# Idle products: their operand zeroed ahead of the masks, more of them at the begin, and a new order table

## The chip, the core and the metric

The kernel runs on one core of a Trainium2 chip. The engines are named PE (TensorE, matmul), DVE (VectorE), ACT (ScalarE), POOL (GpSimd) and SP (SyncE, which here only issues DMAs). The metric is device time in microseconds, the median of several runs.

## What is computed

Three layers follow each other: windowed attention, a gated two-layer product with a shift by one position, and a convolution gate with two products. Batch 4, 8 heads, 576 positions, head size 64; all in float32 (the arrays of q, k, v), weights given as float64 words that the kernel turns into float32 itself.

```python
# attention, window 64
scores = q @ k.transpose(0, 1, 3, 2) / 8
rel = pos[:, None] - pos[None, :]
scores = where((rel >= 0) & (rel < 64), scores, -1e9)
attn = exp(scores - max(scores)); attn = attn / (sum(attn) + 1e-9)
x = (attn @ v) as (4, 576, 512)
# second layer
x_prev = x one position later, 0 at the first
xk = mu_k * x + (1 - mu_k) * x_prev
xr = mu_r * x + (1 - mu_r) * x_prev
x = sigmoid(xr @ w_r) * (maximum(xk @ w_k, 0) ** 2 @ w_v)     # 512 -> 1024 -> 512
# third layer
gate = sigmoid(sum(conv_w[i] * (x shifted by 4 - i) for i in range(5)))
out = (gate * (x @ w_val)) @ w_out                             # 512 -> 512 -> 512
```

## The kernel before

The 2304 positions (4 x 576) are cut into five blocks: block 0 has 256, the others 512. In each block attention runs in four units, one for each pair of heads; units 0 to 3 belong to block 0, unit 4 begins block 1, and there are 20. A unit is: scores on PE (`qk`; in blocks 0 and 1 PE also adds the mask from `low` and `one` by small matmuls, in other blocks DVE does with `cap`), maxima on DVE (`top`, tile `m`), exponentials with their sums on ACT (`exp`, one operation for each 128 columns), reciprocal and norm on DVE (`eps`, `rec`, `norm`, tile `s`), two transposes of the normed scores on PE (`tp0`, `tp`, into PSUM tile `at`), their copies to SBUF on DVE or ACT (`pt`), the product with v on PE (`pv`, also into `at`), and its copy to `xT` on DVE or ACT (`x`). The PSUM tile `at` has two buffers, the scores of units 0 to 3 have two, those of later units one. The scores of units 2 and 3 are computed in the order 3, 2.

When the four units of a block are done, `xT` is mixed with its neighbour (`a`, `xm`), and PE runs the products `r`, `h` and `v`; all of them in three passes over rounded and remaining parts in blocks 1 to 4, in one pass of full float32 on the freshly decoded words of the weights in block 0. The weights come in ten pieces of 1 MB (w_r two, w_k four, w_v four), each loaded by SP into one of four buffers (`x`, `s`, two of `words`), turned into float32 by ACT (`g`, line 337) and DVE (`t`, a shift, line 340, and `s`, the merge, line 342), then split (`hi`, `lo`). A buffer is free for the next piece when DVE has merged the one in it. The third layer follows when the last block is done (from about 328 us on), its products `val` and `out` by a scheme of seven products in place of eight for three batches, plainly for the last.

No scheduler sets the order: every operation is given to `plan.op` or `plan.any` with a cost and what it depends on, and the table `SLOT` gives each a place in one long row, from which each engine gets its own. A letter ahead of a number chooses the engine where there is a choice (`a` ACT, `v` DVE, `p` POOL). `Plan.run` walks that row with the costs only to decide one thing: where PE would stand idle for more than `WAIT` ns at the begin, `fill` puts in products of a zero tile with itself (`warm`, a piece of `sgs`), which nobody reads. It stops doing so when unit 4's scores have been issued. Before, it gives four idle products at the very start and two behind the scores of unit 1. The masks `cap` and `ident` are made on POOL, `low` and `one` from them on DVE, and `warm` is zeroed on POOL behind the masks.

Of the kernel before, what the change touches and what calls it, by code (L numbers as in the profile page):

```python
# [41 lines left out]
    'first': '11',  # L42
    'cap': '4',
    'ident': '8',
    'low': '13',
    'warm': '10',
    'table': '17',
    'ldmu': '2',
    'ldc': '293',
    'mu': '15',  # L50
    'omu': '63',
    'pg': '53',
    'wc0': '451 415 509',
    'wc': '511',
    'first_x': '1',
    'ldqk': '3 5 7 6 20 38 48 85 145 142 179 207 300 319 333 377 374 449 444 476',
    'ldv': '9 24 12 50 76 103 148 168 197 243 297 307 347 370 447 452 473 500 527 596',
    'qk': '16 18 32 27 39 78 110 135 173 196 241 298 329 346 369 413 438 472 499 522',
    'top': '19 21 37 30 49 84 117 143 195 245 301 315 345 365 422 441 466 489 517 543',
    'exp': '22 25 45 34 60 93 123 156 212 262 312 320 349 368 428 454 468 492 519 549',  # L60
    'eps': 'v26 v35 p54 p44 p70 p105 p134 p166 p222 p270 v321 v339 v356 v394 v434 p462 p478 v508 p529 v557',
    'rec': '28 41 58 66 80 126 159 182 225 272 322 341 358 395 435 467 484 510 532 560',
    'norm': '29 46 61 71 99 132 162 191 230 280 323 343 367 403 437 469 495 521 539 566',
    'tp0': '31 52 68 88 108 140 171 204 246 291 327 350 372 418 442 475 501 524 553 586',
    'pt': 'v33 v43 v59 v62 a72 a79 v96 v95 a119 v122 a147 v155 a174 a181 a228 a221 a256 a276 a294 a299 a330 '
        'v336 a355 v363 v390 v393 v427 v431 a448 a465 v493 v487 a516 a515 a533 a536 v555 a563 a619 a634',
    'tp': '36 57 74 90 116 149 178 211 254 295 332 357 389 423 455 485 512 534 559 631',
    'pv': '47 65 83 100 131 163 193 235 282 302 344 366 411 436 470 497 520 541 571 636',
    'x': 'a51 a69 a87 a102 a141 a169 a202 a247 a287 a306 v348 a380 a414 a445 v481 v506 v523 a548 a626 a723',
    'mask': '188 219 283 305 338 361 399 429 459 488 514 537',  # L70
    'edge': '192 226 288 310 340 364 402 432',
    'a': 'a75 a106 a114 a120 a187 a249 a278 a281 a359 v371 a433 v439 a480 v494 v614 a617 v694 a712 a765 a776',
    'xm': '81 112 127 129 266 268 311 286 408 387 450 453 498 502 622 621 696 718 772 780',
    'xlo': '86 115 130 133 275 277 351 296 426 416 474 471 613 611 684 641 763 764 793 783',
    'carry': '138 199 273 342 410 458 507 625',
    'r': '92 118 94 121 97 124 101 128 376 407 400 420 554 562 597 603 720 733 738 750 850 894 877 883',
    'sig': '137 139 146 150 397 417 419 440 575 578 604 612 728 742 751 768 857 898 901 910',
    'h': '154 167 161 186 144 153 158 180 189 214 215 220 208 224 218 231 313 334 324 304 352 360 382 391 486 '
        '504 535 513 546 573 580 590 660 666 687 678 693 702 709 727 823 810 797 830 835 856 863 872',
    'relu': 'a185 a201 a172 a198 a229 a233 a232 a236 v326 v354 v328 a335 a383 a385 a392 v401 a528 a531 v550 v551 '  # L80
# [9 lines left out]
    'shi': '362 378 398 404 538 565 593 600 691 700 721 735 845 858 866 881',  # L90
    'sq': 'v373 a381 a405 v412 a556 a568 a599 a602 a695 a704 v730 a737 a851 v861 v875 a882',
    'staging': '0',
    'w_r ld': '23 40',
    'w_r g': '56 82',
    'w_r t': '64 77',
    'w_r s': '67 91',
# [1103 lines left out]
```

## Time and profile before

| | |
|---|---|
| median of 3 runs | 427.52 us (427.39 to 428.42) |
| the profiled execution | 427.77 us, of which the span of its instructions is 425.7 us |
| PE busy | 413.1 us, 97% of the span |
| DVE busy | 347.1 us, 82% |
| ACT busy | 264.0 us, 62% |
| POOL busy | 25.8 us, 6% |

Matmuls overlap, so a busy PE need not be at its peak; the time from the start of one group of matmuls to the start of the next tells more than their own durations. The clock that a stretch was granted stands in the column PEclk as a share of 2.4 GHz: 1.00 is 2.4 GHz, 0.50 is 1.2 GHz.

### The profile page before, as it was taken

How to read it: one execution, taken by the hardware profiler on the slowest of the kernel's cores; microseconds unless marked ns; L12 is line 12 of the kernel's file. 1: busy time of each engine (PE TensorE's matmuls, PEld its weight loads, DVE VectorE, ACT ScalarE, POOL GpSimd, SP SyncE). 2: the span in 40 equal slices, each digit the busy share in tenths (PEclk: the TensorE clock that was granted, in tenths of full speed). 3: DMA queues.
4: the chain of work that ended last, by engine and by line, in shares of the span. 5: the costliest groups of instructions: out<-in, count | busy, mean ns of one | idle time of the engine just before them, and what ended most of it. 6: DMA issues, size and time to landing. Idle time of an engine off the chain costs nothing.

```text
span 425.7 us, 7996 instructions
## 1 busy us (share of the span) xinstructions
PE 413.1 (97%) x3160; PEld 355.4 (83%) x3160; DVE 347.1 (82%) x506; ACT 264.0 (62%) x596; POOL 25.8 (6%) x66
## 2 busy tenths in 40 slices
PE   5799999999999999999999999999999999999996
PEld 4578888888888888888888888888888999999996
DVE  3889979989898786867597987697667799999970
ACT  4989998668869535867325776165331565668631
POOL 1101101010021000000000000000010000001000
PEclk9889999999999999999999999999999999999999
DMA  6999850553233444034039254177999940417623
GB/s 203 398 417 397 287 216 2 166 151 109 88 105 104 142 134 155 27 93 161 0 143 341 92 183 162 51 260 286 347 407 384 351 141 31 168 28 182 154 111 113
DMA packets 24709, 77.61 MB, mean 182 GB/s; under 512 B 2528, under 2 KB 3296, under 8 KB 22624
## 3 DMA queue, kind: packets, MB, share of 16 engines
q1 hardware_dynamic: 23088, 66.88, 44.5%
q0 software_dynamic: 1440, 10.22, 7.6%
q8 instruction: 25, 0.41, 0.4%
q14 instruction: 12, 0.10, 0.1%
q10 hardware_dynamic: 144, 0.00, 0.0%
HBM read 53.90 MB, written 20.84 MB: 176 GB/s over the span
## 4 chain that ended last, share of the span: by engine, by line
PE 80%; DVE 13%; ACT 2%; DMA 2%; issue 1%; POOL 0%; SPq 0%; ACTq 0%; POOLq 0%
PE h L590 21%; PE v L590 21%; PE r L590 10%; PE at L499 4%; PE at L487 4%; PE qk L425 4%; PE v L613 3%; PE out L965 3%; PE val0m L859 2%; DVE gq L757 2%; PE out2m L859 2%; DMA s<-w_v 2%; DVE x L757 2%; PE h L613 2%; PE r L613 2%; DVE xt L747 2%
## 5 line engine op out<-in xcount | busy, mean ns | idle before, releaser
L590 PE MATMUL h<-x,wk 128*128 128x512 f32 x384 | 91.4, 393 | 0.0
L590 PEld LDWEIGHTS h<-x,wk 128*128 128x128 f32 x384 | 71.2, 188 | 14.6
L590 PE MATMUL v<-sh,wv 128*128 128x512 f32 x256 | 81.7, 392 | 0.0
L590 PEld LDWEIGHTS v<-sh,wv 128*128 128x128 f32 x256 | 48.0, 188 | 9.9
L590 PE MATMUL v<-sl,wv 128*128 128x512 f32 x128 | 49.8, 389 | 0.0
L590 PE MATMUL r<-x,wr 128*128 128x512 f32 x192 | 45.8, 391 | 0.0
L469 ACT ACTIVATE s<-s,m 128x128 f32<-128x128 f32 x96 | 37.4, 396 | 13.1 <-DVE m L458 13.1
L790 DVE SCALAR_TENSOR_TENSOR early<-early,wc 128x576 f32<-128x576 f32 x48 | 38.3, 815 | 5.9 <-ACT early L788 5.3
L590 PEld LDWEIGHTS r<-x,wr 128*128 128x128 f32 x192 | 35.7, 188 | 7.3
L590 PEld LDWEIGHTS v<-sl,wv 128*128 128x128 f32 x128 | 24.1, 188 | 4.8
L670 DVE TENSOR_TENSOR sl<-rk,sh 128x1024 fp32r<-128x1024 f32 x16 | 19.6, 1222 | 8.6 <-ACT rk L668 8.5
L487 PE MATMUL at<-ident,s 128*128 128x128 f32 x144 | 23.9, 287 | 2.1 <-ACT xT L506 1.4
L499 PEld LDWEIGHTS at<-pt,vt 128*64 128x64 f32 x576 | 19.0, 140 | 7.7 <-issue 4.1
L550 DVE SCALAR_TENSOR_TENSOR xm<-xT,omu,xm 128x512 f32<-128x512 f32 x32 | 22.2, 748 | 3.1 <-POOL xT L556 1.6
L487 PEld LDWEIGHTS at<-ident,s 128*128 128x128 f32 x144 | 16.7, 142 | 8.0 <-ACT xT L506 2.3
L499 PE MATMUL at<-pt,vt 128*64 128x64 f32 x576 | 21.9, 228 | 1.2 <-DVE pt L493 1.2
L479 DVE TENSOR_TENSOR s<-s,m 128x1024 f32<-128x1024 f32 (+1 forms) x20 | 22.3, 1114 | 0.2
L425 PE MATMUL qk<-qk 64*64 64x128 f32 x576 | 22.1, 290 | 0.0
L640 ACT ACTIVATE rk<-h 128x512 f32<-128x512 f32 (+1 forms) x30 | 15.4, 535 | 10.2 <-PE h L590 9.2
L794 ACT ACTIVATE early<-early 128x1152 f32<-128x1152 f32 x6 | 7.0, 1170 | 21.9 <-DVE early L790 21.9
L573 DVE TENSOR_TENSOR x<-xm,x 128x1024 fp32r<-128x1024 f32 x16 | 19.2, 1219 | 1.6 <-ACT x L570 1.5
L469 ACT ACTIVATE s<-qk,m 128x128 f32<-128x128 f32 x48 | 16.9, 384 | 4.9 <-DVE m L461 4.9
(178 smaller groups left out, 845.8 us busy)
## 6 DMA issues: line engine op xcount, KB each, us to landing
qk<-qk SPq DMA_DIRECT2D x16, 544.0 KB, 5.6
vt<-vh SPq DMA_DIRECT2D x16, 512.0 KB, 4.8
xb<-x2d SPq DMA_DIRECT2D x4, 1152.0 KB, 7.1
out_t<-st SPq DMA_DIRECT2D x15, 288.0 KB, 2.4
x2d<-sgs SPq DMA_DIRECT2D x16, 256.0 KB, 4.9
w_out<-w SPq DMA_DIRECT2D x8, 512.0 KB, 2.9
w_val<-w SPq DMA_DIRECT2D x8, 448.0 KB, 3.1
wk<-w_val POOLq DMA_DIRECT2D x2, 1792.0 KB, 12.0
```

The source lines that it names most:

```text
L425: PE.matmul(a["ps"][heads[c % 2], h, c // 2 * P:c // 2 * P + P], lhsT=a["q"][heads[h], c * W:(c + 1) * W], rhs=a["k"][heads[h], c * W:c * ...
L469: ACT.activation(out=s, in_=scores()[:, c // n2, c % n2, :] if by_pe else s, func=AF.Exp, scale=D ** -0.5 if by_pe else 1.0, bias=l(0)[:, ...
L479: lambda: V.tensor_tensor(out=a["s"], in0=a["s"], in1=l(1).unsqueeze(2).to_broadcast(sq), op=ALU.mult))
L487: PE.transpose(a["tp", h][:, c * P:(c + 1) * P], a["s"][:, h * n2 + c, :], ident)
L499: PE.matmul(a["o"][heads[h], c * W:(c + 1) * W], lhsT=a["v"][:, c, heads[h]], rhs=a["pt"][:, h, c * W:(c + 1) * W], start=True, stop=True)
L550: V.scalar_tensor_tensor(out=m, in0=xT[:, f, :n], scalar=omu[:, c:c + 1], in1=m, op0=ALU.mult, op1=ALU.add)
L573: lambda E: E.tensor_tensor(out=dst(1), in0=src(), in1=f32(dst(0)), op=ALU.subtract))
L590: PE.matmul(ps, lhsT=a, rhs=b[:, kt, :], start=(kt == 0 and i == 0), stop=(kt == nk - 1 and i == 2))
L613: PE.matmul(Ps[key][:, :n], lhsT=ws(kt), rhs=x()[:, kt, :], start=kt == 0, stop=kt == nk - 1)
L670: lambda E: E.tensor_tensor(out=Ss[t][1][:, f, :n], in0=rk(), in1=f32(Ss[t][0][:, f, :n]), op=ALU.subtract))
L757: lambda E: E.tensor_tensor(out=lo(), in0=src(), in1=f32(hi()), op=ALU.subtract))
L790: V.scalar_tensor_tensor(out=o, in0=x, scalar=c, in1=o, op0=ALU.mult, op1=ALU.add)
```

## The change

The memset of `warm` moves ahead of the masks, and `cap` now names it as something to wait for in the table's walk. The walk assumes a shorter time for an idle product (`PASS` 600 to 430) and that PE may start earlier (`WARM` 900 in place of 1100), so it puts in more of them: six at the start, four behind unit 1's scores, two ahead of unit 4's scores. And the whole table `SLOT` has new numbers, with other choices of engine in some places.

```diff
 SLOT = {
-    'first': '11',
-    'cap': '4',
-    'ident': '8',
+    'first': '32',
+    'warm': '2',
+    'cap': '8',
+    'ident': '5',
     'low': '13',
-    'warm': '10',
...
-    WAIT, PASS = 700, 600
+    WAIT, PASS, WARM = 700, 430, 900
...
             if w[0] == "pe" and self.fill and t - free.get("pe", self.BEGIN) > self.WAIT:
-                self.fill(t, int((t - max(free.get("pe", 0), 1100) - 250) // self.PASS))
+                self.fill(t, int((t - max(free.get("pe", 0), self.WARM) - 250) // self.PASS))
...
     op("first", "pool", 70, [], lambda: G.memset(xT[:, :, 0:1], 0.0))
 
+    warm = sgs[:, 0, :P]
+    op("warm", "pool", 110, [], lambda: G.memset(warm, 0.0))
+
     def masks():
...
-    op("cap", "pool", 1300, [], masks)
+    op("cap", "pool", 1300, ["warm"], masks)
     op("ident", "pool", 600, [], lambda: make_identity(nc, ident))
...
-    warm = sgs[:, 0, :P]
-    op("warm", "pool", 110, [], lambda: G.memset(warm, 0.0))
     op("table", "act", 100, ["warm"], lambda: ACT.activation(out=sgs[:, 1, :1], in_=warm[:, :1], func=AF.Exp), table="exp")
```

The start of POOL's row, the masks and the zeroing of `sgs`; before:

```order
L304 AFFINE_SELECT cap_95<-cap_95 64x128
L306 AFFINE_SELECT cap_95<-cap_95 64x128
L304 AFFINE_SELECT cap_95<-cap_95 64x128
L306 AFFINE_SELECT cap_95<-cap_95 64x128
masks.py:197 MEMSET ident_58 128x128
masks.py:199 AFFINE_SELECT ident_58<-ident_58 128x128
L319 MEMSET sgs_72 128x128
L297 MEMSET xT_98 128x4
```

And now:

```order
L300 MEMSET sgs_72 128x128
masks.py:197 MEMSET ident_58 128x128
masks.py:199 ISA
masks.py:199 AFFINE_SELECT ident_58<-ident_58 128x128
L307 AFFINE_SELECT cap_95<-cap_95 64x128
L309 AFFINE_SELECT cap_95<-cap_95 64x128
L307 AFFINE_SELECT cap_95<-cap_95 64x128
L309 AFFINE_SELECT cap_95<-cap_95 64x128
```

The zeroing went from the seventh place to the first, `ident` ahead of `cap`. Lines below the move are one higher in the changed kernel.

The start of SP's row, the loads; `qk3` is the buffer of units 2 and 3, `vt0` and `vt2` hold v of units 0, 1 and 2, 3. Before:

```order
L398 DMA qk0_122<-qk 128x576 x2
L398 DMA qk3_138<-qk 128x576 x2
L404 DMA vt0_145<-vh 128x512
L404 DMA vt2_149<-vh 128x512
L398 DMA qk4_193<-qk 128x1088
L355 DMA x0_118<-w_r 128x2048
L404 DMA vt0_145<-vh 128x512
L398 DMA qk5_262<-qk 128x1088
L355 DMA s0_119<-w_r 128x2048
```

And now:

```order
L399 DMA qk0_123<-qk 128x576 x2
L399 DMA qk3_144<-qk 128x576 x2
L356 DMA x0_118<-w_r 128x2048
L399 DMA qk4_191<-qk 128x1088
L405 DMA vt0_200<-vh 128x512 x2
L399 DMA qk5_264<-qk 128x1088
L356 DMA s0_119<-w_r 128x2048
L324 DMA cw_62<-conv 128x40
L405 DMA vt2_300<-vh 128x512 x2
```

The first piece of w_r went ahead of unit 4's load (which waits for PE to have read units 0 and 1), the loads of v behind it.

DVE's row from the norm of unit 0 (tile `s0`) on; `m3` and `s3` are those of units 2 and 3, `at0`, `pt0` of unit 0, `at1`, `pt1` of unit 1. Before:

```order
L479 TENSOR_TENSOR s0_197<-s0_197,m0_190 128x512
L460 TENSOR_REDUCE m3_228<-qk3_211 128x4
L461 TENSOR_SCALAR m3_228<-m3_228 128x4
L493 COPY pt0_231<-at0_232 128x256
L474 TENSOR_SCALAR m0_190<-m0_190 128x4
L460 TENSOR_REDUCE m3_228<-qk2_235 128x4
L461 TENSOR_SCALAR m3_228<-m3_228 128x4
L477 RECIPROCAL m0_190<-m0_190 128x4
L493 COPY pt0_231<-at0_257 128x256
L479 TENSOR_TENSOR s0_197<-s0_197,m0_190 128x512
L460 TENSOR_REDUCE m4_308<-qk4_264 128x8
```

And now:

```order
L480 TENSOR_TENSOR s0_195<-s0_195,m0_188 128x512
L461 TENSOR_REDUCE m3_229<-qk3_212 128x4
L462 TENSOR_SCALAR m3_229<-m3_229 128x4
L494 COPY pt0_232<-at0_233 128x256
L494 COPY pt0_232<-at0_237 128x256
L341 TENSOR_SCALAR x0_118<-x0_118 128x1024
L478 RECIPROCAL m0_188<-m0_188 128x4
L461 TENSOR_REDUCE m3_229<-qk2_247 128x4
L462 TENSOR_SCALAR m3_229<-m3_229 128x4
L478 RECIPROCAL m3_229<-m3_229 128x4
L480 TENSOR_TENSOR s0_195<-s0_195,m0_188 128x512
L480 TENSOR_TENSOR s3_242<-s3_242,m3_229 128x512
```

The two copies of unit 0 now follow each other, the shift of w_r's first piece (`x0`) stands behind them, and a norm of units 2 and 3 comes ahead of unit 4's maximum. Further on the same row has the third norm, two copies of unit 1, the merge of w_r, and `xT<-at1`, which was ACT's before. In ACT's row the conversion of w_r's first piece (`g`) moved ahead of the exponentials of unit 2; it stood behind `xT<-at0`. Far behind, three conversions of the last operand of the third layer (`ghi`) went from ACT to DVE.

## Rows read from the trace of the kernel before

**Rows 1.** Busy time of each engine by stretch (us), number of instructions, clock.
```profile
core 0: us, PE busy (x) PEld busy (x) DVE busy (x) ACT busy (x) POOL busy (x), PEclk, DMA share, GB/s
13.00:18.50 5.50, 3.03 (x48) 1.88 (x38) 5.34 (x12) 5.50 (x28) 0.96 (x3) 0.92 1.01 380
18.50:24.50 6.00, 5.90 (x62) 4.53 (x63) 4.82 (x9) 4.32 (x11) 0.59 (x1) 0.50 1.02 419
24.50:60.00 35.50, 35.50 (x443) 29.77 (x441) 31.82 (x45) 34.55 (x107) 4.39 (x8) 1.00 0.90 342
60.00:328.00 268.00, 267.63 (x1797) 220.97 (x1794) 218.41 (x308) 158.28 (x343) 13.85 (x36) 1.00 0.47 162
340.00:400.00 60.00, 58.69 (x433) 57.59 (x432) 59.92 (x89) 40.70 (x65) 3.65 (x5) 1.00 0.43 124
```

**Rows 2.** Timeline of the first 12 us: start, duration, engine, line, operation, [idle before].
```profile
1.07 0.29 POOL L304 TENSOR_SCALAR_AFFINE_SELECT cap<-cap 64x128 f32<-64x128 f32 x1 [0.63 <-DVE cap L300]
2.99 0.21 POOL L319 MEMSET sgs<- 128x128 f32 x1
3.25 2.08 PE L1144 MATMUL idle<-sgs 128*128 128x128 f32 x8 [3.25 <-POOL xT L297]
5.49 1.16 PE L425 MATMUL qk<-qk 64*64 64x128 f32 x16
7.72 0.37 ACT L469 ACTIVATE s<-qk,m 128x128 f32<-128x128 f32 x1 [4.29 <-DVE m L461]
9.26 0.17 DVE L474 TENSOR_SCALAR m<-m 128x4 f32<-128x4 f32 x1 [0.60 <-ACT s L469]
10.43 0.44 PE L487 MATMUL at<-ident,s 128*128 128x128 f32 x2 [0.35 <-DVE s L479]
10.94 0.65 PE L425 MATMUL qk<-qk 64*64 64x128 f32 x16
```

**Rows 3.** The chain of work that ended last, in order of time: start, us.
```profile
18.27 0.28 ACT xT L506
19.29 0.58 PE qk L417 x4
23.90 2.94 PE r L613 x12
30.82 3.46 PE r L613 x16
409.06 12.81 PE out L965 x96
```

**Rows 4.** DVE's groups by form in 0 to 36 us: count, busy, mean ns.
```profile
L460 DVE TENSOR_REDUCE m<-qk 128x8 f32<-128x1024 f32 x3 | 3.7, 1225 | 0.7 <-PE qk L425 0.5
L460 DVE TENSOR_REDUCE m<-qk 128x4 f32<-128x512 f32 x4 | 2.8, 690 | 3.6 <-PE qk L425 3.4
L479 DVE TENSOR_TENSOR s<-s,m 128x512 f32<-128x512 f32 x4 | 2.7, 686 | 0.0
L493 DVE COPY pt<-at 128x256 f32<-128x256 f32 x6 | 2.4, 411 | 0.0
L340 DVE TENSOR_SCALAR x<-x 128x1024 int32<-128x1024 int32 x1 | 0.7, 691 | 0.0
L342 DVE SCALAR_TENSOR_TENSOR words<-words,x 128x1024 int32<-128x1024 int32 x1 | 1.2, 1225 | 0.0
```

**Rows 5.** DMA issues: KB each, us from issue to landing.
```profile
x<-w_r SPq DMA_DIRECT2D x1, 1024.0 KB, 6.0
```

**Rows 6.** Waits: who for whom, us in total, times, longest.
```profile
DVE s L340 <- DMA s<-w_v: 2.3, 1, 2.3
PE at L487 <- DVE s L479: 0.4, 1, 0.4
PE val3m L859 <- DVE early L900: 0.7, 1, 0.7
PE out2m L859 <- ACT x L754: 0.6, 1, 0.6
```

**Rows 7.** Timeline of DVE, its last instruction.
```profile
413.46 0.76 DVE L573 TENSOR_TENSOR gq<-gate,gq 128x576 fp32r<-128x576 f32 x1 [0.75 <-ACT gq L570]
```

240 rows, old and new, of the table SLOT are left out of this document.

## The prediction, made before the run

> **What bounds the kernel now.** I read the busy times by stage first, then the timeline of the first twelve microseconds, then the chain of work that ended last, and at the end the waits.
>
> The stages [rows 1] say where time can be won at all. From 24.5 to 60 us TensorE (PE) is busy for all 35.50 us, from 60 to 328 for 267.63 of 268, from 340 to 400 for 58.69 of 60. The matmuls of the program are the same before and after, apart from the idle products, so these stages can only be made shorter by the few waits in them. What is left is the begin: between 13 and 18.5 us PE is busy for 3.03 of 5.5 us, and before 3.25 us it does nothing [rows 2]. Here the reader should also look at the clock column: 0.92 in 13 to 18.5, 0.50 in 18.5 to 24.5, 1.00 after. 0.92 over 5.5 us is 0.9 us at half rate, so the clock fell to 1.2 GHz at about 17.6 us, after the stretch with gaps, and came back at about 24.5, after six microseconds without a gap (5.90 of 6.00 busy). What stands in those six microseconds ran at half speed.
>
> The same is seen at the very start, where the clock column does not tell it: sixteen score matmuls took 1.16 us at 5.49 and 0.65 us at 10.94 [rows 2]. PE begins at the lower rate too, and the idle products are there to have that spell over sooner.
>
> The chain [rows 3] runs in the begin from PE to DVE to ACT and back. ACT's xT eviction of unit 1 at 18.27 releases the transposes of unit 2, and the fifth unit's scores follow at 19.29; from there the chain stays on PE. So the price of anything in the first 18 us is read at that place: how much earlier does PE get through 19.29?
>
> **The change, step by step.**
>
> *The zeroed operand.* Before, the memset of `sgs` stands behind all masks: it starts at 2.99, takes 0.21, and PE starts at 3.25 [rows 2]. Now it is GpSimd's first work. GpSimd was ready at 0.44 (its first mask at 1.07 had waited 0.63 for DVE's memset of `cap`, which is no condition for `sgs`); somewhere between 0.44 and 1.07 all engines are let go. I take 0.75, so the idle products start at 0.75 + 0.21 + 0.05 = 1.0. Eight matmuls of four products took 2.08 us, 0.26 each; six products are twelve matmuls, 3.1 us, and end at 4.1. The first scores then start at 4.1 in place of 5.33, **1.2 us sooner**. Do the masks still come in time? They take what they took from 1.07 to 2.99, 1.9 us, from 0.96 or 1.07 on, then DVE's two operations on `low` and `one`: about 3.6, ahead of 4.1. If GpSimd were slower by half a microsecond it would still cost nothing; beyond that it costs one for one.
>
> *More idle products behind unit 1 and ahead of unit 4.* Four products (2.1 us at the low rate) now fill the time in which PE waits for the first exponentials. Two units' scores at some 1.05 each (5.33 to 7.4 before, by the 1.16 of the matmuls and what overlaps) end near 6.2, so the idle products end at 8.3 at worst. The next scores are released when unit 0's exponentials end: these began at 7.72, and DVE's next step waited for them until 9.26 [rows 2]; 1.2 sooner is 8.0. Cost between 0 and 0.3 us; I take 0.1, since at the higher rate the four take half. The two products ahead of unit 4 lie in a wait.
>
> *The new order up to 19.29.* DVE is what PE waits for here. Unit 0's first transposes waited for DVE's norm and started at 10.43 [rows 2]; 1.2 earlier, less 0.1, is 9.3, and DVE is free then. What DVE must do from there until unit 1's `x` (now a DVE copy, before ACT's at 18.27): two maxima of 0.69, one of 1.23, three norms of 0.69, the shift of w_r's first piece 0.69, its merge 1.23, four copies of 0.41, which is 1.38 + 1.23 + 2.07 + 0.69 + 1.23 + 1.64 = 8.2 [rows 4], and nine tiny operations at some 0.1 between starts: 9.1 in all, end at 18.4 if nothing overlaps. Copies follow each other by about 0.1 less than they last, so 18.0 is nearer. Before, ACT's copy of 18.27 ended at about 18.55. The scores of unit 5 then start at 18.7 to 18.3 in place of 19.29. I take **0.8 us** sooner, bounds 0.4 and 1.2. The merge of w_r needs the load, which SP now issues ahead of unit 4's scores. Before, it took 6.0 us to land [rows 5]; now it stands right behind the first four loads, and even 7 us behind its issue it is there at about 10, when DVE comes to it. ACT's part (its conversion of w_r moved in between two exponentials) hides in the wait of unit 2's exponentials for their maximum.
>
> *From 19.29 to 35.* PE has no gap there, before and after. What it does at 1.2 GHz costs double: twelve matmuls of `r` took 2.94 us at 23.90, sixteen 3.46 us at 30.82 [rows 3], 0.22 each at full rate. If the clock comes back at the same instant, work that starts 0.8 us sooner at half rate wins only 0.4; if it comes back as long after the gaps end as before, 0.8. I take the mean, **0.6**. The new order runs one half product of `r` (four matmuls, 0.87 us) behind unit 6's scores instead of ahead of them; that moves work and saves none.
>
> *From 35 to 328.* One wait: at 60.4 PE waited 0.4 us for a norm of DVE, and DVE had stood 2.3 us for the last piece of w_v [rows 6]. The loads of the weights begin sooner, and the shift of that piece now stands later in DVE's row. I count the **0.4** as gone; bounds 0 and 0.8, since a new wait can stand elsewhere.
>
> *From 328 on.* Two waits of PE of 0.7 and 0.6 us [rows 6], with DVE busy 59.92 of 60 us [rows 1]. The new order changes which operation comes when in some hundred places; I leave these waits as they are, bounds -1.3 and +2.
>
> Sum: 0.6 + 0.4 = 1.0 us, and 0.3 more for the 1.0 to 1.2 us by which DVE and ACT run ahead and for small waits under 0.3 us in 63 to 67. 1.3 us from the profiled execution's 427.77 is 426.5; the median of the runs lies 0.25 below that execution, so **426.2 us**.
>
> **A rule set beside the clock rows.** The rows: PE ran at half rate from 17.6 to 24.5, after gaps, though it had been at full rate before [rows 1]. The Trainium skill, page "TensorE: Matmul & The Clock Gate", section "HAM oscillation — how this bites in real kernels", says that a PE which goes idle between bursts is throttled anew and pays for warming up each time. By that rule the added idle products buy nothing behind unit 4, since none of them stands in the gaps of 13 to 18.5; the trace agrees in that the four and two products of before did not keep the clock. This is why the forecast keeps the slow spell.
>
> **Rivals.**
> *The slow spell goes or shrinks to a third.* For it: PE's clock is up sooner, and the gaps lie elsewhere. Against: no idle product stands between unit 4's scores and unit 5's, where PE still waits for DVE and ACT. Then the 5.9 us of work of 18.5 to 24.5 take up to 2.9 less; DVE (31.82 of 35.50 busy) and ACT (34.55 of 35.50) [rows 1] let through about 1.5 of it beyond the 0.6. Time 424.7. Chance 0.18.
> *The begin is won and given back.* ACT is 97% busy from 24.5 to 60 [rows 1]. If its row is not also ahead, PE comes sooner and waits before 60 us, and DVE still stands for w_v's last piece. Time 427.3. Chance 0.24.
> *Slower: DVE becomes late in the last stage.* DVE has no idle time between 340 and 400. Its last subtraction starts at 413.46 and takes 0.76 [rows 7], and the products of the last half sequence that need it start near 415.5 (half of 12.8 us behind 409.1): 1.2 us of slack. Three conversions of the last operand move from ACT to DVE, 0.4 to 0.7 each, 1.2 to 2.1 together, though the hop to ACT goes with them. From about 1.2 us of added DVE work or waits each microsecond is one of the kernel; four such, with the begin's 1.0 won, give 429.3. Chance 0.16.
>
> **How the numbers follow.** The forecast has 0.42, with a range of its own of 425.4 to 427.0. A measurement of this kernel can tell 0.3%, 1.3 us, from no change: faster means below 426.24, slower above 428.8. Faster: the first rival 0.18, and of the forecast somewhat over half, 0.26, and 0.04 of luck in the last stage: 0.48. Slower: 0.15. Same: the rest, 0.37. The range takes in the first rival and the second, and stops short of the third: 424.2 to 427.9.
>
> **What would show it.** Right: the idle products start near 1.0, the first scores near 4.1; w_r has landed before 10; unit 5's scores start 0.4 to 1.2 us before 19.29; a stretch of half clock again, ending within 1 us of 24; PE without gaps to 328. Wrong: idle products later than 1.6 (the step on GpSimd fails); scores of unit 5 not sooner than 19.0 (the sum for DVE fails); no stretch at half clock (first rival); waits of PE over 0.5 us between 35 and 76 (second); waits of over 2 us together behind 340 (third).

## The result, and the profile after the change

The changed kernel takes 433.14 us (median of four, 432.54 to 433.87) against 427.79 beside it: a ratio of 1.0126, 95% interval 1.0111 to 1.0140. It is slower by 5.3 us; the forecast of 426.2 lay 1.3 us below the 427.52 then known. The profiled execution took 433.17 us, with a span of 430.6.

Busy time of each engine by stretch, as in [rows 1], after the change:

```profile
core 0: us, PE busy (x) PEld busy (x) DVE busy (x) ACT busy (x) POOL busy (x), PEclk, DMA share, GB/s
13.00:18.50 5.50, 3.57 (x60) 2.46 (x60) 4.15 (x9) 5.07 (x24) 0.40 (x2) 1.00 0.97 334
18.50:24.50 6.00, 4.80 (x49) 3.82 (x50) 5.71 (x11) 5.29 (x22) 0.00 (x0) 1.00 1.00 406
...
60.00:140.00 80.00, 80.00 (x759) 66.30 (x758) 72.61 (x91) 60.41 (x167) 4.65 (x22) 1.00 0.30 96
140.00:160.00 20.00, 18.20 (x155) 14.69 (x155) 14.66 (x22) 14.77 (x46) 0.10 (x1) 1.00 0.56 177
160.00:325.00 165.00, 165.00 (x867) 136.18 (x862) 113.00 (x171) 82.70 (x133) 5.63 (x13) 1.00 0.52 189
325.00:336.00 11.00, 5.93 (x29) 5.42 (x28) 9.18 (x13) 4.13 (x6) 0.22 (x2) 0.84 0.39 115
```

Read it against [rows 1]. In this execution the slow clock of 18.5 to 24.5 is gone (1.00 for 0.50). The other three executions have a mean granted clock of 0.988 to 0.992 over their span (this one 0.996), which is 3.5 to 7 us more at half clock in each; the mean does not say where. The one with the lowest clock took the shortest time, 432.54. From 60 to 328 PE had been busy but for 0.4 us; now 1.8 us are missing between 140 and 160, and between 325 and 336 PE works for 5.93 of 11 us, part of that at half clock. The timeline of the begin, answering to [rows 2]:

```profile
0.73 0.20 POOL L300 MEMSET sgs<- 128x128 f32 x1 [0.29 <-POOLq L1191]
...
0.99 2.93 PE L1145 MATMUL idle<-sgs 128*128 128x128 f32 x12 [0.99 <-POOL sgs L300]
...
5.25 1.16 PE L1145 MATMUL idle<-sgs 128*128 128x128 f32 x8
...
7.35 0.31 PE L418 MATMUL qk<-low,one 64*64 64x256 bf16 x4 [0.94 <-ACT s L470]
```

The first scores stand at 3.85 us, unit 5's at 17.09 (19.22 before in the same view), the product of unit 4 with v at 31.14 (34.20 before). So the loss is behind it, and the waits of PE (who for whom, us in total, times, longest) say where, beside [rows 6]:

```profile
PE val0m L860 <- DVE x L758: 5.1, 1, 5.1
PE at L488 <- DVE s L480: 1.3, 2, 0.8
PE at L500 <- DMA vt<-vh: 1.2, 1, 1.2
...
PE at L500 <- ACT pt L493: 1.0, 1, 1.0
...
PE val3m L860 <- ACT early L872: 0.7, 1, 0.7
...
PE out2m L860 <- DVE gq L758: 0.3, 1, 0.3
```

The last two answer to the 0.7 and 0.6 of [rows 6]; the first is new, and so are one wait of 0.8 in the second line, the 1.2 for a load of v, which lies in the begin, and the 1.0. To follow them through all runs, *lost time* below is the length of a stretch less what the matmuls that start in it take one behind the other at full clock (0.227 us each for `r`, `h`, `v`, 0.134 for `val`, `out`, and so on). The short matmuls of attention overlap, so a figure can be off by some tenths. Added up from the start it is:

| up to, us | 35 | 140 | 160 | 325 | 335 | end |
|---|---|---|---|---|---|---|
| before | 14.1 | 13.9 | 13.8 | 13.7 | 13.7 | 16.2 |
| after | 10.7 | 10.3 | 12.1 | 12.1 | 19.0 | 21.1 |

The begin won 3.4 us, 3.6 by 140. The stretch 140 to 160 took back 1.9, the ten microseconds behind 325 another 6.9. With 0.3 won in small pieces that makes 4.9, the difference of the two spans.

For the large one, the waits of all engines from 300 to 345 and then the chain that ended last (start, us, what) lead from PE back to a load:

```profile
POOL wol L1119 <- ACT early L795: 9.8, 1, 9.8
ACT x L755 <- DMA xb<-x2d: 8.8, 2, 7.7
ACT early L789 <- DMA gd<-early: 8.2, 1, 8.2
...
DVE xt L748 <- DMA xb<-x2d: 5.9, 2, 5.1
```

```profile
294.56 9.77 issue
304.87 17.73 DMA xb<-x2d
322.73 0.76 DVE xt L748
323.48 0.71 DVE x L758
```

`xb` is x of the third layer's first batch (`load`, op `ldx`). GpSimd zeroes its padding, then SyncE loads 1.18 MB into it. Before, this load left at 294.82 and landed at 300.69, ahead of all six loads of w_val and w_out. Now it leaves at 304.87 and takes 17.73 us. The rows that wait for `xb<-x2d` show why it matters: VectorE and ScalarE need it for the splits that the first product of the third layer reads, PE stops at 326.35 until 331.70, and then runs 3.4 us at half clock.

### The profile page after: what moved, and what is told of

It reads as the page before. It is cut to its first block, busy times and chain, and to the rows that moved or that the text cites. A ratio compares the mean times of both kernels' runs of the same rounds, so it can differ in the third digit from the quotient of the medians.

```text
span 430.6 us, 8009 instructions
## 1 busy us (share of the span) xinstructions
PE 413.3 (96%) x3172; PEld 356.5 (83%) x3172; DVE 341.7 (79%) x500; ACT 266.3 (62%) x602; POOL 19.1 (4%) x68
## 4 chain that ended last, share of the span: by engine, by line
PE 68%; DVE 16%; DMA 10%; issue 4%; ACT 1%; SPq 1%; ACTq 0%; POOL 0%; POOLq 0%; DVEq 0%
PE h L591 20%; PE v L591 14%; PE r L591 8%; DMA xb<-x2d 6%; PE at L500 4%; PE at L488 4%; PE qk L426 3%; PE h L614 3%; PE v L614 3%; PE out L966 3%; DVE x L758 3%; DVE xt L748 2%; PE out2m L860 2%; DVE gq L758 2%; DMA vt<-vh 2%
## 5 line engine op out<-in xcount | busy, mean ns | idle before, releaser
L488 PE MATMUL at<-ident,s 128*128 128x128 f32 x144 | 22.9, 279 | 3.0 <-DVE s L480 1.3
L641 ACT ACTIVATE rk<-h 128x512 f32<-128x512 f32 (+1 forms) x31 | 15.8, 535 | 12.1 <-PE h L591 11.9
L493 ACT ACTIVATE pt<-at 128x512 f32<-128x512 f32 (+1 forms) x30 | 16.4, 560 | 9.3 <-PE at L488 9.2
L665 ACT ACTIVATE sh<-rk 128x1024 fp32r<-128x1024 f32 x16 | 16.7, 1057 | 8.2 <-DVE rk L643 8.1
L426 PE MATMUL qk<-qk 64*64 64x128 f32 x576 | 20.3, 274 | 0.0
```

The lines of the kernel that those rows point to most:

```text
L426: PE.matmul(a["ps"][heads[c % 2], h, c // 2 * P:c // 2 * P + P], lhsT=a["q"][heads[h], c * W:(c + 1) * W], rhs=a["k"][heads[h], c * W:c * ...
L488: PE.transpose(a["tp", h][:, c * P:(c + 1) * P], a["s"][:, h * n2 + c, :], ident)
```

## The experiments

Each row has the kernel before run beside it; ratios with 95% intervals. A ratio is not always the quotient of the two medians, which for wk0_behind would be 1.0210. A profile shows one execution, not the median one: those of tail_back_all and mid_rows are the slowest of their twelve and ten, that of after_to_32_us the second slowest of twelve, that of after_then_before the fastest of five, and those of idle_only, small_rows and small_rows_taps the second fastest of ten.

| kernel | median us | before | ratio |
|---|---|---|---|
| the change | 433.14 | 427.79 | 1.0126 (1.0111 to 1.0140) |
| ldx_early | 436.87 | 427.17 | 1.0227 (1.0204 to 1.0250) |
| wol_behind | 432.87 | 427.17 | 1.0136 (1.0113 to 1.0158) |
| idle_only | 426.28 | 427.17 | 0.9979 (0.9964 to 0.9995) |
| table_only | 434.93 | 427.17 | 1.0182 (1.0167 to 1.0197) |
| wk0_behind | 436.91 | 427.91 | 1.0177 (1.0113 to 1.0241) |
| tail_back | 426.76 | 427.91 | 0.9984 (0.9964 to 1.0005) |
| before_then_after | 437.06 | 427.91 | 1.0214 (1.0182 to 1.0246) |
| after_then_before | 424.70 | 427.91 | 0.9933 (0.9908 to 0.9958) |
| few_bytes | 429.46 | 427.39 | 1.0034 (1.0009 to 1.0060) |
| tail_back_taps | 426.35 | 427.39 | 0.9970 (0.9952 to 0.9989) |
| after_to_32_us | 427.15 | 427.39 | 0.9991 (0.9973 to 1.0009) |
| small_rows | 425.67 | 427.24 | 0.9971 (0.9948 to 0.9994) |
| tail_back_all | 425.89 | 427.24 | 0.9958 (0.9936 to 0.9980) |
| after_then_before_again | 425.44 | 427.24 | 0.9955 (0.9938 to 0.9972) |
| mid_rows | 428.21 | 427.11 | 1.0025 (1.0008 to 1.0043) |
| small_rows_taps | 425.09 | 427.11 | 0.9956 (0.9938 to 0.9974) |

**ldx_early: the load put back ahead, a miss.**

```diff
-    'ldx': '896 944 960 1012',
+    'ldx': '875 944 960 1012',
```

> The changed kernel with one number of its table put back ahead: the load of x for the third layer's first batch moves from 896 to 875, in front of the two early gate commands on SyncE and of the four loads of w_out on GpSimd, behind the two loads of w_val. Theory A (this load is what the changed kernel lost its time to: it left at 304.87 and landed at 322.60, TensorE stopped for 5.36 us at 326.3 and then ran 3.41 us at half clock): the load leaves at about 294.6, right behind the two w_val loads, and lands by 309 (3.67 MB of theirs took 12.9 us, with 1.18 MB more it is some 17); no stop at 326, no half clock: 433.14 - 5.36 - 1.7 = 426.1, range 425.3 to 426.9. Theory B (VectorE and ScalarE are late there anyway and the load only came last in the list of waits): the stop shrinks by no more than 2 us, 431 or more. Theory C (the traffic of the w_val and w_out loads stretches it wherever it is put): it lands after 315, a stop of 1 to 4 us stays, 428 to 432.

It became slower. x left at 294.70 and landed at 310.92, 11.7 us sooner; but the waits from 300 to 330 show another transfer in its place:

```profile
DVE early L791 <- ACT early L789: 19.2, 1, 19.2
ACT early L789 <- DMA gd<-early: 17.4, 1, 17.4
...
PE v L591 <- ACT sgs L681: 5.9, 1, 5.9
```

The early gate's store (`gd`, 0.59 MB, SyncE) left at 304.33 and landed at 322.56. ScalarE's next tap wants the buffer it reads, and the eviction of the second layer's products is queued behind that tap. From 311 to 320 us VectorE and ScalarE did nothing at all and the DMA engines moved 414 GB/s. Theory A is wrong as it was put: a place in the row is not enough, there are two small transfers that are wanted there, x and the store, and moving one ahead sent the other to the end.

**wol_behind: GpSimd's wait alone.**

```diff
-    'wo2': '901 902 900 894',
+    'wo2': '901 902 900 897',
```

> The changed kernel, but on GpSimd alone the zeroing of xb stands ahead of all loads of w_out (the one of them that stood ahead moves from 894 to 897); on SyncE the load of x stays where it was, behind the early load (which left at 302.75 after 11.6 us of waiting) and the early store. Theory A1 (the 9.79 us that GpSimd waits for room for w_out, with the zeroing queued behind, are the cause): the zeroing runs at about 294.6, the load follows at once, 426.1. Theory A2 (both queues hold the load: SyncE's two commands ahead of it also leave only at 302.75 and 303.92): the zeroing runs at 294.6 but the load still leaves at 304.3 or later and lands at about 322: 432.5 to 433.5.

432.87, as A2 said: the zeroing ran at 292.79, and the load left at 303.03, since SyncE's early load ahead of it left at 300.98. So SyncE's queue alone holds it. That GpSimd's would too is read from the changed kernel, where the zeroing stands at 304.86, behind the 9.8 us; no run frees SyncE alone.

**tail_back and wk0_behind: the order of the loads.**

```diff
-    'wv2': '870 873',
+    'wv2': '903 873',
...
-    'ldx': '896 944 960 1012',
+    'ldx': '875 944 960 1012',
```

wk0_behind has only the first of the two edits.

> The changed kernel; only one of the two loads of w_val on GpSimd (1.83 MB, left at 293.28) goes behind the loads of w_out, where it stood in the kernel before (870 to 903). The load of x stays where it is (304.87). Theory C1 (bytes in flight: from 293 to 325 the 16 DMA engines are busy without a break, at 411 GB/s by the windows of ldx_early, and whatever is issued into it lands late): the bytes in flight behind 304.9 stay nearly the same, x lands at 318 to 322, a stop of 2 to 5 us stays: 429 to 433. Theory C2 (the w_val pair alone is what x shares with): x lands before 315, no stop: 426.

> Both moves together on the changed kernel: x ahead of the early gate's commands and of the w_out loads (896 to 875, as in ldx_early) and one w_val load behind them (870 to 903), so that one w_val load, x, the w_out loads and the other w_val load follow each other as in the kernel before. Theory C1 (two small transfers are wanted in that stretch, x by about 317 and the early gate's store by about 313, and both were stuck in the flood of 7.9 MB of weights): x leaves at about 294.7 beside one w_val load and lands by 305, the store leaves at 304.3 and lands by about 313 as in the changed kernel; no stop from 310 to 335, no half clock: 433.1 - 7.1 = 426.0, range 425.3 to 427.0. Rival (the early gate's chain on ScalarE is late by itself): the stop of ldx_early at 312 to 320 comes back, 430 or more.

tail_back took 426.76, within the range: x left at 294.62 and landed at 305.26, the store took 7.20 us and landed at 311.43. All that PE waited for from 300 to 345 was

```profile
PE val0m L860 <- DMA wk<-w_val: 1.3, 1, 1.3
```

and the clock stayed at 1.00. With x left in its late place, wk0_behind was no better: by the medians 3.8 us above the changed kernel, with one of its four executions at 432.80, and by the ratio not clear of it. In its profile, the slowest of the four, x landed at 327.32, 22.52 us after it left, and PE waited 5.8 and 3.2 us. The range of 429 to 433 was too low: what was moved behind x left at 306.86 and was under way beside it all the same.

**before_then_after and after_then_before: one half of the row from each kernel.** The first has the order of before up to number 860, the second that of the change up to 400; what is left follows in the other kernel's order, with 2000 added to its numbers. One line of after_then_before against the changed kernel:

```diff
-    'qk': '15 16 35 25 45 76 111 137 185 215 247 304 331 350 383 415 452 475 506 543',
+    'qk': '15 16 35 25 45 76 111 137 185 215 247 304 331 350 383 2413 2438 2472 2499 2522',
```

> The kernel before, begin and all, up to number 860 of its order (some 280 us); from there what is left is done in the order of the changed kernel. Theory C1 (the order of the last loads is enough to make the stop, whatever went before): the stop of 5.4 us at about 328 and the half clock behind it come: 427.2 + 7.1 = 434.3, range 432.5 to 435.5. Rival (it takes the changed kernel's other moves too, its earlier second layer): 427 to 430.

> The changed kernel, idle products and all, up to number 400 of its order (some 108 us); from there what is left is done in the order of the kernel before. By the lost time of TensorE the begin won 3.9 us by 76 us, and nothing between there and 108; the waits of 140 to 160 (2.0) and of 325 to 335 (7) belong to later numbers. So 427.2 - 3.9 = 423.3, range 422.6 to 424.3, faster than both. Rival (what the begin won is waited for again later in the old order, at a transfer or at a slower engine): 425.5 to 427.2.

before_then_after: 437.06, above its range of 432.5 to 435.5. PE waited 6.0 us for `val0m` and 1.0 for an eviction, x landed at 325.92, the clock fell behind the stop. So the order of the last numbers, the loads with all else behind 860, is enough to make the loss. after_then_before: 424.70, and 425.44 in its second measurement below: 1.8 to 3.2 us faster than before, less than the 3.9 forecast, and outside the first range. Its waits of PE from 20 to 400 us are two, as in [rows 6]:

```profile
PE val3m L848 <- DVE early L889: 0.7, 1, 0.7
PE out2m L848 <- ACT x L743: 0.6, 1, 0.6
```

**after_to_32_us: the same cut at number 140.**

> As after_then_before, but the changed kernel's order only up to number 140 (about 32 us), the rest in the order of the kernel before. By the lost time of TensorE the changed kernel had won 3.3 of its 3.9 us by 35 us: 427.5 - 3.3 = 424.2, range 423.4 to 425.4, within 0.7 us of after_then_before. Rival (the new order between 32 and 108 us carries a part of the gain, or the old one there gives it back): 426 or more.

427.15, no gain: the rival was right. Between 33 and 78 us PE waited

```profile
PE h L602 <- DVE words L331: 1.7, 1, 1.7
PE at L476 <- DVE s L468: 0.5, 1, 0.5
```

The lost time from 35 to 76 is 2.5 us, where the changed kernel has -0.3. This profile also has the longest spell of half clock of all with the change's begin, 6.8 us from 16.34. By the medians (427.15 beside 424.70 and 425.44 for after_then_before) the new order between 32 and 108 us is a part of the gain. That it is so by bringing the pieces of the weights to VectorE in time is argued from these waits and was not run by itself.

**idle_only and table_only: the two parts of the change.** idle_only is the kernel before with the memset of `warm` ahead of `masks`, its place in the row, and

```diff
-    'warm': '10',
+    'warm': '2',
...
-    WAIT, PASS = 700, 600
+    WAIT, PASS, WARM = 700, 430, 900
...
-    op("cap", "pool", 1300, [], masks)
+    op("cap", "pool", 1300, ["warm"], masks)
```

table_only is the changed kernel with these put back, `warm` at 8 and `idle` at 9.

> The kernel before with the idle part of the change alone: the zeroed operand first on GpSimd, 6 and 4 idle products where 4 and 2 stood, the order table as before (but for the zeroing). First scores at 3.9 instead of 5.33, -1.2 to -1.5. Theory 1 (the half clock of the kernel before from 17.66 to 24.49 comes of the order of the work up to there, whenever the clock rose): it stays, 427.79 - 1.3 = 426.5, range 426.0 to 427.0. Theory 2 (it comes of the late rise of the clock at 7.42; with the rise at about 4 it goes): a further 6.83 us at half speed are won back, as far as TensorE was the bound there, 1.5 to 3: 423.5 to 425.

> The changed kernel without the idle part: the operand zeroed behind the masks as before, 4, 2 and 1 idle products, the new order of everything else. The load of x stays late, so the stop at 326 and its half clock stay. Theory 1 (the new order alone keeps the clock up between 17.7 and 24.5): the clock rises at about 7.4 and stays; only the first scores are 1.2 to 1.5 later: 433.14 + 1.3 = 434.4, range 434.0 to 435.0. Theory 2 (the early rise keeps it up): a half-speed spell of some 3 to 7 us comes back in the begin, 435.5 to 437.5.

idle_only won 0.9 us (0.2 to 1.5), less than the 1.3 of theory 1; its profiled execution has half clock from about 17.2 to 20.6 us, 3.4 us in place of 6.8. The old begin has that as well, without the idle part: the profile of before_then_after has 3.4 us, from 18.77. table_only has no half clock in the begin, and is 1.8 us above the changed kernel (by the ratios, 2.4): unit 4's product with v stands at 32.36, 1.2 later, and at the stop of 326 the clock was low for 6.8 us instead of 3.4. In this profile, then, the spell is gone without the added idle products. That the order took it out is not shown: of the thirteen other profiles with the change's begin four have 3.4 us of it and one 6.8. The idle part is worth 0.9 us in the one comparison and about 2 in the other.

**few_bytes, small_rows and mid_rows: why a load on its way takes 18 us.** Edits of GpSimd's loads; few_bytes, then small_rows (mid_rows has 1024 in place of 512):

```diff
-           lambda c=c: G.dma_start(out=flat(wk[c])[:, :14 * 256], in_=flat4(wd["w_val", c])), moves=1.25 * 14 * 256)
+           lambda c=c, n=14 * 256 if c else 256: G.dma_start(out=flat(wk[c])[:, :n], in_=flat4(wd["w_val", c])[:, :n]), moves=1.25 * 14 * 256)
...
-               lambda c=c, j=j: G.dma_start(out=Q["wol", j] if c else flat(wr[j]),
+               lambda c=c, j=j: G.dma_start(out=Q["wol", j] if c else flat(wr[j])[:, :256],
```

```diff
+           lambda c=c: [G.dma_start(out=flat(wk[c])[:, o:o + 512], in_=flat4(wd["w_val", c])[:, o:o + 512])
+                      for o in range(0, 14 * 256, 512)], moves=1.25 * 14 * 256)
...
+               lambda c=c, j=j: [G.dma_start(out=(Q["wol", j] if c else flat(wr[j]))[:, o:o + 512],
+                                               in_=flat4(wd["w_out", c])[:, j * 2048 + o:j * 2048 + o + 512])
+                               for o in range(0, 2048, 512)], moves=1.25 * 2048)
```

> The changed kernel with all its loads in place and in order, but three of them on GpSimd bring only 256 of their columns (one w_val load 256 of 3584, the two loads of the high part of w_out 256 of 2048), so what the third layer multiplies with is mostly left over from the layer before and the output isn't the reference's; every instruction of TensorE, VectorE and ScalarE stays. 3.5 of the 7.9 MB of weights are gone; the zeroing of xb still stands behind the wait for room (9.79 us). Theory C1 (bytes in flight): x still leaves at about 304.9 but lands by 313 instead of 322.60, the stop of 5.36 and the half clock go: 433.1 - 7.1 = 426.0, range 425.0 to 427.2. Theory A1 (leaving at 304.9 is already too late): a stop of 2 us or more stays, 428.5 or more.

> The changed kernel with all its bytes and its order, but GpSimd's six loads of weights go out in pieces of 512 columns, so that a partition's row in them is 2 KB instead of 8 or 14 KB; the rows of x and of the early gate's store, on SyncE's queue, are 2.3 KB. Theory D (between 300 and 326 the two queues shared the 16 engines by rows, 721 packets of 8.2 KB against 1600 of 2.2 KB, so that SyncE's queue got 3.54 of 9.49 MB and its small wanted transfers waited for the large ones): SyncE's share grows to about half of 411 GB/s; the early gate's store lands by 310 instead of 312.99, x (zeroed up to 2 us later, as GpSimd has four pieces to issue ahead) by 316 instead of 322.60, the stop of 5.36 us falls to 1 or less: 426 to 427.5. Theory C1 (only the sum of bytes counts): x lands at 321 to 325 as before, 432 to 435.

> small_rows with pieces of 1024 columns: rows of 4 KB on GpSimd's queue, between the 2 KB of small_rows and the 8 and 14 KB of the changed kernel. In small_rows GpSimd waited 10.0 us in sum for its own earlier pieces before it issued the next (eight were under way at most), so what helped there may have been the pacing and not the rows; here the eight pieces of w_out all go out at once. Theory D (shares by rows): in between: the early gate's store lands 6 to 8 us after it left (9.07 in the changed kernel, 4.88 in small_rows), x at 315 to 320, a stop of 0 to 3 us, 426 to 430. Theory P (pacing alone): nothing is paced from 304 on, the store takes 9 us, x lands at 321 or later, 431 to 434.

few_bytes leaves out 3.5 MB of the weights. Its time, 429.46, and its waits of PE, 1.7 and 0.6 us, are those of its theory A1; but x left at 304.71 and landed at 319.43, so it took 14.72 us instead of 17.73, and the stop shrank. The store alone took 10.02 us, as the two loads of w_out that were left whole stood beside it. So the bytes beside a load count, but 3.5 MB less of them did not bring x in by 313 as C1 had it. small_rows, with every byte back and the order of the change, took 425.67: no stop at 326 at all. The DMA queues from 300 to 321 (packets, MB, share of 16 engines; us to landing), first of the changed kernel, then of mid_rows, then of small_rows; q0 holds GpSimd's loads, q1 SyncE's:

```profile
q0 software_dynamic: 716, 5.92, 71.9%
q1 hardware_dynamic: 1026, 2.28, 31.4%
...
xb<-x2d SPq DMA_DIRECT2D x1, 1152.0 KB, 17.7
...
gd<-early SPq DMA_DIRECT2D x1, 576.0 KB, 9.1
```

```profile
q0 software_dynamic: 1356, 4.67, 63.1%
q1 hardware_dynamic: 1326, 2.94, 42.8%
...
xb<-x2d SPq DMA_DIRECT2D x1, 1152.0 KB, 15.3
...
gd<-early SPq DMA_DIRECT2D x1, 576.0 KB, 7.0
```

```profile
q0 software_dynamic: 2075, 3.78, 59.2%
q1 hardware_dynamic: 1600, 3.54, 50.8%
...
xb<-x2d SPq DMA_DIRECT2D x1, 1152.0 KB, 11.8
...
gd<-early SPq DMA_DIRECT2D x1, 576.0 KB, 4.9
```

GpSimd's packets shrink from 8.3 to 3.4 and 1.8 KB (MB by packets), SyncE's stay at 2.2, and SyncE's part of the bytes grows from 28 to 39 to 48%. The store and x land sooner in the same steps, and the time falls from 433.14 to 428.21 to 425.67. mid_rows has no pacing of GpSimd's loads behind 304 and still won 4 to 5 us (4.3 by the ratios), so pacing alone is out. x landed there at 320.07, at the late end of what sharing by rows expected. In small_rows x left 2.1 us sooner than in mid_rows, the w_val pieces had landed by 303.63 (305.83 in mid_rows), and the last loads of w_out left only as earlier ones landed. So how much of the last step comes from the rows stays open.

**tail_back_taps, tail_back_all and small_rows_taps: the rest of the loss.** At 140 to 160 ScalarE's timeline of the changed kernel (start, duration, operation, [idle before]) reads

```profile
143.82 0.58 ACT L493 ACTIVATE pt<-at 128x512 f32<-128x512 f32 x1
147.96 1.44 ACT L789 ACTIVATE early<-early,wc 128x576 f32<-128x576 f32 x2 [3.56 <-DMA early<-x2d]
149.31 0.57 ACT L493 ACTIVATE pt<-at 128x512 f32<-128x512 f32 x1
```

The early gate's load leaves at 140.67 in the new order (164.90 before) and lands at 147.87. ScalarE's first tap waits 3.56 us for it, and a copy of unit 15 that PE needs stands behind.

```diff
-    'rec': '26 39 63 46 96 115 147 187 231 280 321 345 377 410 440 464 500 533 563 571',
+    'rec': '26 39 63 46 96 115 147 187 231 280 321 345 377 410 440 464 493 533 563 571',
...
-    'norm': '27 47 66 51 100 126 170 201 236 287 322 346 380 411 445 470 505 535 566 586',
+    'norm': '27 47 66 51 100 126 170 201 236 287 322 346 380 411 445 470 493 535 566 586',
...
-        'a338 v378 a374 v393 a407 a421 v443 a462 a469 a496 a489 a514 a522 v544 a556 a581 a579 v618 a638',
+        'a338 v378 a374 v393 a407 a421 v443 a462 a469 a490 a489 a514 a522 v544 a556 a581 a579 v618 a638',
```

tail_back_all has `'wv2': '897 873'` besides.

> tail_back with three numbers more: at 140 to 160 the copy of unit 15's weights on ScalarE goes ahead of the first two taps of the early gate (496 to 490), and unit 16's reciprocal and normalisation on VectorE ahead of all but one of these taps (500 and 505 to 493). In the changed kernel the early gate's load leaves at 140.67 (164.90 in the kernel before) and lands at 147.87; ScalarE waits 3.56 us for it with the copy queued behind, VectorE 2.66, and TensorE waits 0.96 and 0.84. Theory (queued behind a load): both waits go, the lost time of 140 to 160 falls from 1.6 to under 0.4, tail_back's 426.8 beside a kernel before of 427.9 becomes 425.5, range 424.5 to 426.5, ratio 0.992 to 0.997. Rival (the values for the product at 150, which landed at 149.4, or the early gate's later taps hold TensorE instead): lost time of 1 us or more stays, no difference to tail_back.

> tail_back_taps with its second w_val load ahead of three of the four w_out loads (903 to 897; still behind x), since in tail_back_taps TensorE's one stop after 300 and before 385 was for that load: 1.6 us at the first product of the third layer, it landed at 326.56. It should land at about 317, x at 304 as there, the w_out loads by 328 (wanted by the first gated product, some 15 us later): no stop, 426.35 - 1.6 = 424.8, range 423.8 to 425.8, ratio 0.991 to 0.996. Rival (the early gate's store or a w_out load is late instead): 426 or more.

> after_then_before once more, beside tail_back_all on one chip. By its first measurement (0.9933, 0.9908 to 0.9958) 424.5, range 423.5 to 425.5; tail_back_all within 0.5 us of it, as both have the changed begin and neither the early gate's load ahead of its time nor the late loads.

> small_rows with the three numbers of tail_back_taps at 140 to 160 (the waits there lost 0.76 us in small_rows): its order is otherwise the changed kernel's. 425.67 beside a kernel before of 427.24 becomes 424.9, range 424.0 to 425.9, ratio 0.992 to 0.997. It would be the changed order without its losses, within 0.6 us of after_then_before. Rival (the taps moved behind press on something later): 425.7 or more.

In tail_back_taps PE waits for nothing between 130 and 165, and the lost time of 140 to 160 is -0.1 (1.6 in tail_back): the theory of that wait holds. The whole kernel shows less of it, 0.997 against 0.998, with intervals that overlap. tail_back_all took the 1.6 us of the w_val load away, but in its profiled execution the early gate is late instead, as its rival said (its store took 8.22 us, PE waits 2.4 us for `early`, until 335.57, and the clock is low from 335.18 for 3.4 us); this execution, 427.24, is the slowest of its twelve, 423.86 to 427.24. after_then_before in its second measurement, tail_back_all and small_rows_taps end alike, at 0.9955 to 0.9958, which is 1.8 to 1.9 us less than before. None of the three can be told from the others.

## Why the prediction was wrong, step by step

*The zeroed operand* was right: idle products at 0.99 (forecast 1.0), first scores at 3.85 (4.1). They start just where the load of unit 0's q and k, which left at 0.74, lands; all profiles with the idle part have 3.85 or 3.86. The forecast did not name this load, so the good fit is in part luck. *More idle products* cost nothing: the clock was up by 4.1, they took 1.16 us, and PE then waited 0.94 for the exponentials.

*The new order up to unit 5's scores* was mis-sized: 2.1 us sooner instead of 0.8. Half of the difference is there at unit 0's first transposes, which stand at 8.59 (forecast 9.3), the other half in the 9.1 us summed for VectorE, which took 8.5 from there to 17.09.

*From 19.29 to 35* failed. "PE has no gap there" did not hold: PE waited 1.16 us, until 19.59, for v of units 2 and 3, whose load now left at 11.34 (3.06 before). And the slow spell was kept in the forecast because no idle product stands in the gaps; in the changed kernel's profile the clock stayed at 1.00, although PE was busy for only 3.57 of 5.5 us before. The first rival (424.7, chance 0.18) was nearer: 3.4 us of lost time less by 35, where it had 2.1 and the forecast 0.6. But the spell comes and goes between executions of one kernel (none in the first profile of after_then_before, 3.4 us in the second), so part of that is luck. By the profiles that share a begin:

| order of the begin | half clock in it, us | profiles | unit 4's product with v at, us |
|---|---|---|---|
| before | 6.8 | before | 34.20 |
| before | 3.4 | before_then_after | 33.32 |
| the change | 6.8 | after_to_32_us | 32.86 |
| the change | 3.4 | few_bytes, mid_rows, tail_back_taps, after_then_before_again | 31.69 to 31.92 |
| the change | none | the change itself and the eight others that have its idle part | 30.13 to 31.82 |

With a like spell on both sides the change's begin is 1.3 to 1.6 us ahead there, more than the 0.6 that was forecast, and less than the 3.1 of the two single profiles.

*From 35 to 328* failed: w_v's wait of 0.4 went as counted, but two waits of 1.8 us together came at 149 and 152, outside the bound of 0.8. *From 328 on* is the step that decided: "I leave these waits as they are, bounds -1.3 and +2". Of the waits it named the 0.7 stayed and the 0.6 became 0.3. What decided was a new one: x of the third layer's first batch left 10.05 us later and took 17.73 us instead of 5.87, PE stopped for 5.1 us and then ran 3.4 us at half clock. The prediction weighs the new order on PE, VectorE and ScalarE, and not that `ldx` had moved behind a waiting load on GpSimd and behind the early gate on SyncE, nor that both w_val loads and one of w_out had come ahead of x, where all six had stood behind it, four of them as late as 309 to 311. The third rival was slower for a wrong reason: VectorE's last subtraction starts at 417.78, 8.7 us ahead of the last matmul, as it did before (8.1).

What is shown: the order of the last numbers makes the loss by itself (before_then_after), putting two loads back takes it away (tail_back), and so do smaller rows with the order unchanged (small_rows). What is not: why the profile of tail_back_all has the early gate late, and how the gain of the begin, 3.4 to 3.6 us of lost time in the changed kernel's profile, becomes 1.8 to 3.2 in the medians. The table above goes a part of the way: one profile stands beside another with and without the spell. The profiled begins of kernels that share it also spread: lost time up to 35 us is 9.6 in wol_behind, 10.0 and 11.5 in the two profiles of after_then_before, 11.3 in tail_back.

## What to carry to other kernels

When a change rewrites an order, walk the DMA issues of every queue as closely as the engines' rows: for each load, what stands ahead of it, what that waits for, and which other transfers leave in the same ten microseconds. An early operation that waits for a transfer in an in-order row (a convolution tap here) delays everything behind it, so it is moved ahead only as far as its transfer is. Where a small wanted transfer must share the DMA engines with large ones that are not urgent, smaller rows for the large ones gave it a larger share here, without touching the order. Before a difference between two profiles is explained, look at how far the executions of one kernel differ: here a spell of half clock that one profile had and the next had not.

## What the runs showed of the hardware that I had not expected

SyncE's queue got a larger share of what the DMA engines moved when GpSimd's packets were smaller: 28, 39 and 48% of the bytes from 300 to 321 us with GpSimd's packets at 8.3, 3.4 and 1.8 KB and its own at 2.2. SyncE's first transfer there left at 302.76, 303.01 and 300.91, so a part of this is a later start. From 306 to 319, when both queues had work all the time, its share was 27, 47 and 51%: the step is that from the changed kernel to mid_rows. The Trainium skill, page "DMA: Bandwidth & Descriptors", section "Queues, rings and completion order", says that an engine goes round the queues that have work, a whole packet at a time. The traces agree in direction, but not one for one: from 306 to 319 SyncE's packets beside GpSimd's are 613 beside 507, 995 beside 670 and 1050 beside 1232. The page's packet holds several descriptors, and whether what the profile counts as a packet is the same unit is not shown here.

Half clock is not always paid. Two kernels with the same begin, by stretch: tail_back first, then tail_back_taps.

```profile
16.00:20.00 4.00, 2.00 (x44) 1.39 (x42) 2.69 (x5) 3.90 (x15) 0.20 (x1) 1.00 1.02 372
20.00:24.50 4.50, 4.39 (x47) 3.48 (x48) 4.47 (x9) 3.88 (x20) 0.00 (x0) 1.00 1.00 414
```

```profile
16.00:20.00 4.00, 3.03 (x42) 2.15 (x40) 3.21 (x6) 3.95 (x15) 0.20 (x1) 0.58 1.03 395
20.00:24.50 4.50, 4.38 (x52) 3.37 (x47) 4.17 (x8) 3.52 (x19) 0.00 (x0) 1.00 1.01 415
```

One ran at full clock, the other at 0.58 from 16 to 20 us, and unit 4's product with v began at 31.69 in both. PE waited for others there, so its slower matmuls filled a wait. Whole executions agree. Of the six of after_then_before_again three have a mean granted clock of 0.999 and three of 0.996, so some 3 us more at half clock; they took 425.31 to 425.45 and 425.44 to 425.58. Of the 95 executions of the kernel before that ran beside the later kernels five have 1.000, so no such spell at all, and they lie 0.9 below to 0.1 above the medians beside them. Why the clock falls in one execution and not in the next stays open. One thing went before it: in the nine profiles without the spell full clock began between 3.89 and 6.01 us, in four of the five with it between 6.10 and 7.02, in mid_rows at 3.99. Behind 326, at the stops of 5.1 to 6.0 us (the change, wol_behind, table_only, before_then_after), the granted clock fell to 0.50 for 3.4 to 6.8 us; at those of 1.3 to 2.3 us (tail_back, tail_back_taps, few_bytes, mid_rows) it stayed at 1.00, but at the one of 2.4 us in tail_back_all it was 0.50 from 335.18 to 338.59.
